# Attention, then a gated feed-forward block: output weights loaded between q and v of batch 1, half of the output of batch 0 as partial sums beside attention 1, q of batches 2 and 3 in one buffer

## The chip, the cores and the metric

One core of one Trainium2 chip runs the whole program. The time is that of one execution on the device in microseconds; the number that counts is the median of the runs of a kernel. "Clock" is the share of TensorE's full clock that was granted. PE is TensorE, DVE VectorE, ACT ScalarE, POOL GpSimd and SP SyncE; POOL and SP here do little but issue DMAs, each in order on its own queue.

## What is computed

Eight batches, 8 heads, 576 positions of 64 numbers, 32 memory slots. The slots are weighted sums of k and v, the queries attend to them, and the 4608 x 512 result goes through a gated feed-forward block:

```python
a = softmax(phi, over the 32 slots)            # [b, h, s, m]
k_m = einsum('bhsm,bhsd->bhmd', a, k)
v_m = einsum('bhsm,bhsd->bhmd', a, v)
attn = softmax(q @ k_m^T / sqrt(64))           # [b, h, s, m]
x = (attn @ v_m), heads side by side           # [4608, 512]
out = (silu(x @ w_gate) * (x @ w_val)) @ w_out # 512 -> 1536 -> 512
```

## The kernel before

**Tiles.** The kernel works batch by batch. The 32 slots of 4 heads fill 128 partitions, so a batch has two groups of heads. `k_items`, `v_items` and `kv_items` sum k and v with the exponentials of phi (`phi_exp`, on ACT) and transpose the sums (`kv_T`). `scores` multiplies them with the transposed q and takes E = exp on ACT. `z_inv` sums E over the slots on PE and takes Ln and Exp on ACT. `norm` multiplies E by that on DVE (t_A). `u_round` multiplies v_m with the columns of w_gate and w_val (t_U), evicted half by ACT and half by DVE, so that x itself is never made.

**Slots.** `gv_slots` has 24 slots for each batch. A slot makes 288 columns of gate and of value for one of the 12 blocks of d_ff, four matmuls in all; ACT takes Silu of the gate and DVE multiplies it with the value into t_h.

**Output units.** `out_units` makes an output tile of 128 rows from 12 matmuls, called units here, one for each block of d_ff, into a PSUM tile of pool `po` (two buffers), evicts it by DVE or ACT (t_o, three buffers) and stores it by two DMAs on SP. An even batch gives 4 such tiles, an odd one 5. They wait in the list `backlog`. At the start of each batch from 2 on, 2 + 8 + 14 + 12 = 36 units are taken between the steps of attention; `rest` is spread among the 24 slots by `spread`, which sorts by a position given by hand. Before, `rest` leaves 36 units in the list in each batch but the last; batch 1 has 12 units beside its slots, batches 2, 4 and 6 have 24, batches 3 and 5 have 12, and batch 7 has 48. The last 60 units run alone.

**Loads.** Weights, phi, k, v and q come through POOL's queue. An issue there waits until the eighth issue ahead of it has landed, and for its buffer to be free. q has two buffers that take turns. From batch 2 on q is transposed by a DMA on SP (`load_qT`); q of batches 0 and 1 by PE (`q_T`). The program text is the order on each engine. `preload_act_table_set` loads a function table on ACT (ACT_TABLE_LOAD).

**Attention 1** is what stands between the slots of batch 0 and those of batch 1. Here no output units run before.

Of the kernel before, what the change touches and what calls it, by code (L numbers as in the profile page):

```python
# [9 lines left out]
FP32 = mybir.dt.float32  # L10
BF16 = mybir.dt.bfloat16
# [3 lines left out]
def kernel(  # L15
# [17 lines left out]
    nc = tc.nc  # L33
    AF = mybir.ActivationFunctionType
    ALU = mybir.AluOpType

    B, H, S, D = q.shape
    M = phi.shape[3]
    DM, DF = moe_w_gate.shape
    P, J = 96, 6  # L40
    NG = 2
    NP = H // 2
    NJF = DF // 128
# [7 lines left out]
    inp = ctx.enter_context(tc.tile_pool(name="inp", bufs=2))  # L51
# [3 lines left out]
    work = ctx.enter_context(tc.tile_pool(name="work", bufs=3))  # L55
    ps = ctx.enter_context(tc.tile_pool(name="ps", bufs=6, space=bass.MemoryType.PSUM))
    po = ctx.enter_context(tc.tile_pool(name="po", bufs=2, space=bass.MemoryType.PSUM))
# [4 lines left out]


    phis, kvs, qs, qTs = {}, {}, {}, {}

    def load_phi(b, eng):
        t = inp.tile([P, H, J * M], FP32, tag="phi", name="t_phi")
        eng.dma_start(out=t, in_=phi[b].rearrange("h (p j) m -> p h (j m)", p=P))  # L68
        phis[b] = t
# [6 lines left out]
    def load_v(b):  # L76
        nc.gpsimd.dma_start(
            out=kvs[b][:, 1], in_=v[b].rearrange("h (p j) d -> p h (j d)", p=P)
        )

    def load_q(b):
        t = inp.tile([P, H, J * D], BF16, tag="q", name="t_q")
        nc.gpsimd.dma_start(out=t, in_=q[b].rearrange("h (p j) d -> p h (j d)", p=P))  # L83
        qs[b] = t

# [27 lines left out]
    WO = {}  # L113

    def load_wo(c):
        t = wpool.tile([128, 4, DM], BF16, tag=f"WO{c}", name=f"WO{c}")
        nc.gpsimd.dma_start(
            out=t,
            in_=moe_w_out[c * CH:(c + 1) * CH, :].rearrange("(i p) f -> p i f", p=128),
        )  # L120
        for i in range(4):
            WO[4 * c + i] = t[:, i]
# [9 lines left out]
    def phi_exp(b):  # L132
        t = att.tile([P, J, NG, NP, M], BF16, tag="ephi", name="t_ephi")
        src = phis.pop(b).rearrange("p (i g) (j m) -> p g i j m", g=NG, m=M)
        for g in range(NG):
            nc.scalar.activation(  # L136
                out=t[:, :, g].rearrange("p j i m -> p i j m"), in_=src[:, g], func=AF.Exp
            )
        ephis[b] = t
# [45 lines left out]
    def v_norm(b, p):  # L185
        bv = att.tile([128, NG, D], BF16, tag="bv", name="t_bv")
        nc.vector.tensor_tensor(
            out=bv,
            in0=p,
            in1=rSs[b].rearrange("p g a c -> p g (a c)").to_broadcast([128, NG, D]),  # L190
            op=ALU.mult,
        )
        bvs[b] = bv
# [43 lines left out]
    def v_items(b):  # L237


        def sums():  # L240
            p = ps.tile([128, NG * D], FP32, tag="b", name="p_kv")
            kv_sum(b, p, (1,))
            v_norm(b, p.rearrange("p (g d) -> p g d", g=NG))

        return [sums, lambda: kv_T(b, (1,))]
# [20 lines left out]
    def gv_banks():  # L266
        return [
            ps.tile([128, CH], FP32, tag="b", name=f"p_{'gv'[r]}") for r in range(2)
        ]

    def scores(b, g):
        p = gv_banks()
        for i in range(NP):
            for r in range(2):
                nc.tensor.matmul(  # L275
                    p[r][32 * i:32 * i + 32, 0:HALF],
                    lhsT=kTs[b][64 * r:64 * r + 64, g, 32 * i:32 * i + 32],
                    rhs=qTs[b, i][64 * r:64 * r + 64, g],
                    start=True,
                    stop=True,  # L280
                    tile_position=(64 * r, 32 * i),
                )
        e = att.tile([128, 2, HALF], BF16, tag=f"E{g}", bufs=1, name="t_E")
        for r in range(2):
            nc.scalar.activation(out=e[:, r], in_=p[r][:, 0:HALF], func=AF.Exp, scale=sm_scale)  # L285
        es[b, g] = e
# [15 lines left out]
    def norm(b, g):  # L302
        a = att.tile([128, 2, HALF], BF16, tag=f"A{g}", name="t_A")
        nc.vector.tensor_tensor(out=a, in0=es.pop((b, g)), in1=lzs.pop((b, g)), op=ALU.mult)  # L304
        atts[b, g] = a
# [33 lines left out]
    hts = {}  # L339
# [48 lines left out]
            t += n  # L388
        return segs

    def out_units(c, u, eng):

        mine = {}

        def unit(jf):
            def run():
                if jf == 0:
                    mine["p"] = po.tile([128, DM], FP32, tag="o", name="p_oo")
                nc.tensor.matmul(  # L399
                    mine["p"],  # L400
                    lhsT=hts[c, jf][:, 128 * u:128 * (u + 1)],
                    rhs=WO[jf],
                    start=(jf == 0),
                    stop=(jf == NJF - 1),
                )
                if jf == NJF - 1:
                    t_o = work.tile([128, DM], FP32, tag="to", name="t_o")
                    if eng == "a":
                        nc.scalar.copy(out=t_o, in_=mine["p"])  # L409
                    else:  # L410
                        nc.vector.tensor_copy(out=t_o, in_=mine["p"])  # L411
                    for (r0, n, bb, jj, pp) in token_segments(2 * c * S + 128 * u, 128):
                        nc.sync.dma_start(
                            out=out_r[bb, jj, pp:pp + n, :], in_=t_o[r0:r0 + n, :]
                        )

            return run

        return [unit(jf) for jf in range(NJF)]

    def out_list(b):
        tiles = range(0, 4) if b % 2 == 0 else range(4, 9)
        res = []
        for n, u in enumerate(tiles):
            res += out_units(b // 2, u, "v" if n % 4 != 3 else "a")
        return res
# [9 lines left out]
    def u_both_halves(b, c, half, evac="avav"):  # L436

        both = ((0, c, (half,)), (1, c, (half,)))
        return lambda: u_round(b, both, evac)
# [4 lines left out]
    def run(items):  # L444
        for x in items:
            x()
# [33 lines left out]
    for c in range(NCH):  # L480
        for half in range(2):
            for which in range(2):
                load_w(which, c, half)
    load_phi(2, nc.gpsimd)
    load_k(1)
    load_q(1)
    load_v(1)
    for c in range(3):
        load_wo(c)


    exp_tables()
# [22 lines left out]


    exp_tables()
    phi_exp(2)
    run(k_items(1)[:2])
    warm(8)  # L520
    run(q_items(1)[:2] + k_items(1)[2:] + q_items(1)[2:])
    load_q(2)
    load_k(2)
    load_v(2)
    load_phi(3, nc.gpsimd)
    load_q(3)
    for g in range(NG):
        scores(1, g)
    for g in range(NG):
        z_inv(1, g)  # L530
    run(v_items(1))
    norm(1, 0)
    run([u_both_halves(1, 0, 0, "vava")])
    nc.scalar.preload_act_table_set("silu_and_others")
    norm(1, 1)
    backlog = out_list(0)

    def take(n):
        nonlocal backlog
        n = max(0, min(n, len(backlog)))  # L540
        part, backlog = backlog[:n], backlog[n:]
        return part

    for b in range(1, B):
        last = b + 1 == B
        if b > 1:
            exp_tables()
            run(take(2))
            for g in range(NG):
                scores(b, g)  # L550
            if not last:
                load_k(b + 1)
                load_v(b + 1)
            if b + 2 < B:
                load_phi(b + 2, nc.gpsimd)
                load_q(b + 2)
            run(take(8))
            if not last:
                phi_exp(b + 1)
            for g in range(NG):  # L560
                z_inv(b, g)
            nc.scalar.preload_act_table_set("silu_and_others")
            run(take(14))
            norm(b, 0)
            norm(b, 1)
            run(take(12))
        rest = take(len(backlog)) if last else take(len(backlog) - 36)
        g = gv_slots(b)
        streams = [(g, 0, 24), (rest, 0, 24)]
        if b == 1:  # L570
            streams += [
                ([u_both_halves(1, 0, 1)], 1, 2),
                ([u_item(1, 1)], 5, 6),
                ([u_item(1, 2)], 10, 11),
            ]
        else:
            streams += [([u_item(b, 2)], 5, 6)]
        if not last:
            n = 6 if b == 1 else 0
            streams += [  # L580
                ([lambda: load_qT(b + 1)], n, n),
                (kv_items(b + 1), 15, 19) if b == 1 else (kv_items(b + 1), 8, 14),
                ([u_item(b + 1, 0)], 18, 20) if b == 1 else ([u_item(b + 1, 0)], 15, 17),
                ([u_item(b + 1, 1)], 21, 23),
            ]
        spread(*streams)
        flush_mul()
        backlog += out_list(b)
# [31 lines left out]
```

## Time and profile before

| what | value |
|---|---|
| median of 3 runs | 271.58 us (270.94 to 271.93) |
| the profiled execution | 270.88 us |
| its span, first to last instruction | 269.1 us |
| mean granted clock | 0.946 |
| PE busy | 246.0 us (91%) |
| ACT busy | 171.0 us (64%) |
| DVE busy | 152.2 us (57%) |
| DMA written, in 48336 packets | 37.00 MB |

The times of rows are microseconds from the start of the span. The two strips show the span in 40 slices of 6.7 us each; a digit is a share in tenths, for PE of busy time, for PEclk of the full clock:

```profile
PE   7576997798829999999999999999999999999993
PEclk9955999689968999999999999999999999999998
```

Slices 7 to 12 cover 40 to 81 us: attention 1, batch 1 and the start of batch 2. Busy time of PE holds the modelled end of each matmul, so a full slice may still have small gaps.

### The profile page before, as it was taken

The numbers are of one execution on the slowest core, as the hardware profiler recorded it, in microseconds if no ns is written. First come the engines' busy times: TensorE is split into PE (matmuls) and PEld (weight loads), VectorE is DVE, ScalarE is ACT, GpSimd is POOL, SyncE is SP. The second block draws the span as 40 slices with busy tenths as digits, with TensorE's granted clock in tenths as the row PEclk, the third lists the DMA queues.
The fourth block names the chain that finished last, engine by engine and source line by source line (L and its number), as shares of the span: only waits on it lengthen the run. The fifth ranks groups of instructions, "written<-read, shape, count | busy, mean of one in ns | idle before, by whom it ended". The sixth has DMA issues, their size and how long they took to land.

```text
span 269.1 us, 6537 instructions
## 1 busy us (share of the span) xinstructions
PE 246.0 (91%) x2574; PEld 146.2 (54%) x2574; DVE 152.2 (57%) x337; ACT 171.0 (64%) x371; POOL 35.9 (13%) x52
## 2 busy tenths in 40 slices
PE   7576997798829999999999999999999999999993
PEld 7442665356404575556645665566556654566541
DVE  0116893576902677558845685478646873565321
ACT  3257788865827556976797568867985677544200
POOL 8435523200022021100210300000000000000000
PEclk9955999689968999999999999999999999999998
DMA  7999999999999979967988596270135102312143
GB/s 150 226 198 196 220 201 206 205 226 144 168 197 174 284 102 181 164 170 128 147 158 221 82 212 126 58 150 0 41 95 115 39 9 72 80 39 73 46 118 78
DMA packets 48336, 37.00 MB, mean 137 GB/s; under 512 B 15921, under 2 KB 42801, under 8 KB 48305
## 3 DMA queue, kind: packets, MB, share of 16 engines
q0 software_dynamic: 27744, 23.01, 54.2%
q1 hardware_dynamic: 20560, 13.57, 23.5%
q8 instruction: 20, 0.33, 0.5%
q14 instruction: 12, 0.09, 0.1%
HBM read 42.47 MB, written 9.44 MB: 193 GB/s over the span
## 4 chain that ended last, share of the span: by engine, by line
PE 69%; DMA 28%; issue 1%; POOL 0%; DVE 0%; POOLq 0%
PE p_oo L399 34%; PE p_g L352 14%; PE p_v L352 13%; DMA t_qT<-t_q 9%; DMA t_kv<-in_k_dram 8%; DMA t_kv<-in_v_dram 6%; DMA W<-in_moe_w_gate_dram 5%; PE p_u L318 3%; PE p_kv L150 1%; PE p_g L275 1%; PE p_kv L162 1%; PE p_g L295 1%; PE p_v L295 1%; POOL t_phi L68 0%; DVE t_o L411 0%
## 5 line engine op out<-in xcount | busy, mean ns | idle before, releaser
L399 PE MATMUL p_oo<-WO,t_h 128*128 128x512 bf16 x432 | 120.1, 385 | 0.0
L368 ACT ACTIVATE t_sg<-p_g 128x288 bf16<-128x288 f32 x192 | 76.9, 415 | 49.8 <-PE p_g L352 46.7
L375 DVE TENSOR_TENSOR t_h<-t_sg,p_v 128x288 bf16<-128x288 bf16 x192 | 84.5, 451 | 35.6 <-PE p_v L352 32.3
L352 PEld LDWEIGHTS <-t_U 128*128 128x128 bf16 x768 | 73.9, 100 | 44.9 <-issue 9.2
L352 PE MATMUL p_g<-t_A,t_U 128*128 128x288 bf16 x384 | 81.3, 294 | 2.7 <-DVE t_A L304 2.1
L352 PE MATMUL p_v<-t_A,t_U 128*128 128x288 bf16 x384 | 79.6, 291 | 0.0
L399 PEld LDWEIGHTS <-t_h 128*128 128x128 bf16 x432 | 42.1, 99 | 36.6 <-issue 4.7
L411 DVE COPY t_o<-p_oo 128x512 f32<-128x512 f32 x28 | 19.3, 688 | 43.7 <-PE p_oo L399 43.7
L336 DVE CAST t_U<-p_u 128x512 bf16<-128x512 f32 (+1 forms) x57 | 32.1, 605 | 1.5 <-PE p_u L318 0.7
L334 ACT CAST t_U<-p_u 128x512 bf16<-128x512 f32 (+1 forms) x55 | 26.3, 530 | 7.5 <-PE p_u L318 7.1
L136 ACT ACTIVATE t_ephi<-t_phi 96x768 bf16<-96x768 f32 x16 | 12.6, 844 | 8.6 <-DMA t_phi<-in_phi_dram 8.6
L318 PE MATMUL p_u<-W,t_kT 64*32 64x512 bf16 (+1 forms) x448 | 16.8, 365 | 0.6 <-DVE t_kT L206 0.6
L83 POOL DMA_DIRECT2D t_q<-in_q_dram x8 | 6.2, 773 | 69.7 <-DMA t_qT<-t_q 66.0
L304 DVE TENSOR_TENSOR t_A<-t_E,t_lz 128x576 bf16<-128x576 bf16 x16 | 11.7, 753 | 3.5 <-ACT t_lz L299 3.5
L409 ACT COPY t_o<-p_oo 128x512 f32<-128x512 f32 x8 | 4.7, 585 | 13.6 <-DMA out_dram<-t_o 10.0
L299 ACT ACTIVATE t_lz<-t_lz 128x576 f32<-128x576 f32 x16 | 10.9, 683 | 0.5
L275 PE MATMUL p_g<-t_qT,t_kT 64*32 64x288 bf16 x64 | 5.1, 321 | 6.3 <-DMA t_qT<-t_q 5.9
L458 ACT ACT_TABLE_LOAD x8 | 10.3, 1283 | 0.9 <-PEq L604 0.7
L285 ACT ACTIVATE t_E<-p_g 128x288 bf16<-128x288 f32 x16 | 6.6, 414 | 6.5 <-PE p_v L275 6.4
L467 PE MATMUL p_oo<-bones 128*128 128x128 bf16 x118 | 8.4, 239 | 1.5 <-DVE bones L478 1.5
L170 DVE RECIPROCAL t_rS<-p_kv 128x2 f32<-128x2 f32 x8 | 1.4, 171 | 14.8 <-PE p_kv L162 14.8
L318 PEld LDWEIGHTS <-t_kT 64*32 64x32 bf16 x448 | 4.5, 89 | 9.1 <-issue 6.6
(42 smaller groups left out, 133.6 us busy)
## 6 DMA issues: line engine op xcount, KB each, us to landing
t_kv<-in_k_dram POOLq DMA_DIRECT2D x8, 576.0 KB, 9.6
t_q<-in_q_dram POOLq DMA_DIRECT2D x8, 576.0 KB, 9.5
t_kv<-in_v_dram POOLq DMA_DIRECT2D x8, 576.0 KB, 13.1
out_dram<-t_o SPq DMA_DIRECT2D x24, 192.0 KB, 2.3
t_phi<-in_phi_dram POOLq DMA_DIRECT2D x7, 576.0 KB, 11.7
out_dram<-t_o SPq DMA_DIRECT2D x24, 128.0 KB, 2.4
W<-in_moe_w_gate_dram POOLq DMA_DIRECT2D x6, 256.0 KB, 12.9
W<-in_moe_w_val_dram POOLq DMA_DIRECT2D x6, 256.0 KB, 11.8
```

The lines of the kernel that those rows point to most:

```text
L136: nc.scalar.activation(out=t[:, :, g].rearrange("p j i m -> p i j m"), in_=src[:, g], func=AF.Exp)
L299: nc.scalar.activation(out=lz, in_=lz, func=AF.Exp, scale=-1.0)
L304: nc.vector.tensor_tensor(out=a, in0=es.pop((b, g)), in1=lzs.pop((b, g)), op=ALU.mult)
L318: nc.tensor.matmul(p[g][32 * i:32 * i + 32, f0:f1], lhsT=kTs[b][64 * g:64 * g + 64, 2, 32 * i:32 * i + 32], rhs=W[which, c][64 * g:64 * g ...
L334: nc.scalar.copy(out=t, in_=p)
L336: nc.vector.tensor_copy(out=t, in_=p)
L352: nc.tensor.matmul(p[:, 0:HALF], lhsT=Us[b, which, c, g][:, 128 * o:128 * (o + 1)], rhs=atts[b, g][:, r], start=(g == 0), stop=(g == NG - 1),)
L368: nc.scalar.activation(out=sg, in_=gate, func=AF.Silu)
L375: nc.vector.tensor_tensor(out=dst, in0=sg, in1=val, op=ALU.mult)
L399: nc.tensor.matmul(mine["p"], lhsT=hts[c, jf][:, 128 * u:128 * (u + 1)], rhs=WO[jf], start=(jf == 0), stop=(jf == NJF - 1),)
L411: nc.vector.tensor_copy(out=t_o, in_=mine["p"])
L458: nc.scalar.preload_act_table_set("natural_log_exp_and_others")
```

## The change

There are four parts.

1. **Load order.** k and q of batch 1 are issued first, then output weights 0 and 1, phi of 2, v of 1, output weight 2. k and v of batch 2 now stand ahead of q of batch 2.
2. **q's buffers.** `Q_SLOT` gives each batch its buffer: batches 0, 2, 3, 5 and 7 use one, batches 1, 4 and 6 the other. q of 3 therefore waits until the transpose of q of 2 has read that buffer.
3. **Output of batch 0.** The first 8 units of output tiles 0 and 1 run in attention 1 (`out_part`); the sum is copied to SBUF by DVE (t_part). The other 4 units run later, and DVE adds the two on eviction. Of tiles 2 and 3 the first 8 units run in attention 1 and the rest in batch 1. phi's exponentials for batch 2 and the table for Silu move behind `z_inv`.
4. **Lists.** `rest` now takes all that is left in `backlog` in each batch, so batch 1 has 16 units beside its slots and batch 7 has 12. The transpose of q of 2 moves from position 6 to 12 of batch 1.

```diff
+    Q_SLOT = (0, 1, 0, 0, 1, 0, 1, 0)
...
-        t = inp.tile([P, H, J * D], BF16, tag="q", name="t_q")
+        t = inp.tile([P, H, J * D], BF16, tag=f"q{Q_SLOT[b]}", bufs=1, name="t_q")
...
-    def out_units(c, u, eng):
+    def out_units(c, u, eng, first=0):
...
-                    if eng == "a":
+                    if first:
+                        nc.vector.tensor_tensor(
+                            out=t_o, in0=mine["p"], in1=parts.pop(u), op=ALU.add
+                        )
+                    elif eng == "a":
...
+    def out_part(u, count):
+        mine = {}
+        def unit(jf):
+            def run():
+                if jf == 0:
+                    mine["p"] = po.tile([128, DM], FP32, tag="o", name="p_oo")
+                nc.tensor.matmul(
+                    mine["p"],
+                    lhsT=hts[0, jf][:, 128 * u:128 * (u + 1)],
+                    rhs=WO[jf],
+                    start=(jf == 0),
+                    stop=(jf == count - 1),
+                )
+                if jf == count - 1:
+                    parts[u] = work.tile([128, DM], FP32, tag=f"part{u}", bufs=1, name="t_part")
+                    nc.vector.tensor_copy(out=parts[u], in_=mine["p"])
...
-    phi_exp(2)
     run(k_items(1)[:2])
     warm(8)
     run(q_items(1)[:2] + k_items(1)[2:] + q_items(1)[2:])
-    load_q(2)
     load_k(2)
     load_v(2)
+    load_q(2)
     load_phi(3, nc.gpsimd)
     load_q(3)
     for g in range(NG):
         scores(1, g)
+    p0, p1 = out_part(0, 8), out_part(1, 8)
+    t2, t3 = out_units(0, 2, "v"), out_units(0, 3, "a")
+    run(p0[:4] + p1[:4])
     for g in range(NG):
         z_inv(1, g)
-    run(v_items(1))
+    phi_exp(2)
+    nc.scalar.preload_act_table_set("silu_and_others")
+    run(p0[4:] + p1[4:])
     norm(1, 0)
+    norm(1, 1)
+    run(t2[:8] + t3[:3] + v_items(1)[:1] + t3[3:6] + v_items(1)[1:] + t3[6:8])
     run([u_both_halves(1, 0, 0, "vava")])
-    nc.scalar.preload_act_table_set("silu_and_others")
-    norm(1, 1)
-    backlog = out_list(0)
+    backlog = t2[8:] + t3[8:] + out_units(0, 0, "v", 8) + out_units(0, 1, "v", 8)
...
-        rest = take(len(backlog)) if last else take(len(backlog) - 36)
+        rest = take(len(backlog))
...
-            n = 6 if b == 1 else 0
+            n = 12 if b == 1 else 0
```

What this does to the order on POOL, from the last gate and value weights on, is seen in these rows (t_kv holds k and v of a batch, WO0 to WO2 are the output weights; the numbers tell the buffers of one name apart). Before:

```order
L68 DMA t_phi_124<-in_phi_dram 96x8x192
L73 DMA t_kv_126<-in_k_dram 96x8x384
L83 DMA t_q_128<-in_q_dram 96x8x384
L77 DMA t_kv_126<-in_v_dram 96x8x384
L117 DMA WO0_131<-in_moe_w_out_dram 128x4x512
L117 DMA WO1_133<-in_moe_w_out_dram 128x4x512
L117 DMA WO2_135<-in_moe_w_out_dram 128x4x512
L83 DMA t_q_960<-in_q_dram 96x8x384
L73 DMA t_kv_962<-in_k_dram 96x8x384
L77 DMA t_kv_962<-in_v_dram 96x8x384
L68 DMA t_phi_965<-in_phi_dram 96x8x192
L83 DMA t_q_967<-in_q_dram 96x8x384
```

The same twelve places now:

```order
L74 DMA t_kv_124<-in_k_dram 96x8x384
L84 DMA t_q_126<-in_q_dram 96x8x384
L118 DMA WO0_128<-in_moe_w_out_dram 128x4x512
L118 DMA WO1_130<-in_moe_w_out_dram 128x4x512
L69 DMA t_phi_132<-in_phi_dram 96x8x192
L78 DMA t_kv_124<-in_v_dram 96x8x384
L118 DMA WO2_135<-in_moe_w_out_dram 128x4x512
L74 DMA t_kv_957<-in_k_dram 96x8x384
L78 DMA t_kv_957<-in_v_dram 96x8x384
L84 DMA t_q_960<-in_q_dram 96x8x384
L69 DMA t_phi_962<-in_phi_dram 96x8x192
L84 DMA t_q_964<-in_q_dram 96x8x384
```

Two output weights have gone ahead of phi of 2 and v of 1, and q of 2 (t_q_960 in both) has gone behind k and v of 2. The last row is q of 3, which now waits for the transpose of q of 2.

On SP the stores and the transposes stand in one queue. Its first rows before (the first is phi of batch 0, t_qT_1204 is q of 2 transposed):

```order
L68 DMA t_phi_87<-in_phi_dram 96x8x192
L89 DMA_TRANSPOSE t_qT_1204<-t_q_960 128x24x96
L413 DMA out_0_dram<-t_o_1525 96x512
L413 DMA out_0_dram<-t_o_1525 32x512
L413 DMA out_0_dram<-t_o_1609 64x512 x2
```

And now:

```order
L69 DMA t_phi_87<-in_phi_dram 96x8x192
L419 DMA out_0_dram<-t_o_1207 32x512
L419 DMA out_0_dram<-t_o_1207 96x512
L419 DMA out_0_dram<-t_o_1325 96x512
L419 DMA out_0_dram<-t_o_1325 32x512
L90 DMA_TRANSPOSE t_qT_1338<-t_q_960 128x24x96
```

The four stores of output tiles 2 and 3 now stand ahead of the first transpose.

On PE, from the last matmul of the scores of batch 1 to its first slot (the rows of t_E are the sums over the slots, p_kv the sums of v, p_T their transpose, p_u0 a U round, p_g and t_A a gate), before:

```order
L275 MATMUL p_v_983<-t_qT_929,t_kT_940 32x288
...
L295 MATMUL p_g_995<-t_E_979,bones_85 128x288
...
L150 MATMUL p_kv_1011<-t_kv_126,t_ephi_141 32x64
...
L200 MATMUL p_T_1062<-ident_84,t_bv_1060 128x128
...
L318 MATMUL p_u0_1067<-W00_106,t_kT_940 32x256
...
L352 MATMUL p_g_1098<-t_A_1065,t_U_1077 128x288
```

And now, up to the U round, with the first row of each group of output matmuls (p_oo, the first two the partial sums):

```order
L276 MATMUL p_v_980<-t_qT_926,t_kT_937 32x288
...
L437 MATMUL p_oo_992<-WO0_128,t_h_488 128x512
...
L437 MATMUL p_oo_997<-WO0_128,t_h_488 128x512
...
L296 MATMUL p_g_1002<-t_E_976,bones_85 128x288
...
L437 MATMUL p_oo_992<-WO1_130,t_h_612 128x512
...
L401 MATMUL p_oo_1038<-WO0_128,t_h_488 128x512
...
L401 MATMUL p_oo_1047<-WO0_128,t_h_488 128x512
...
L151 MATMUL p_kv_1051<-t_kv_124,t_ephi_141 32x64
...
L401 MATMUL p_oo_1047<-WO0_128,t_h_593 128x512
...
L201 MATMUL p_T_1105<-ident_84,t_bv_1100 128x128
...
L319 MATMUL p_u0_1110<-W00_106,t_kT_937 32x256
```

Between the scores and the U round 32 output matmuls have come in: 8 ahead of the sums over the slots, 8 + 8 + 3 behind them, and 3 + 2 beside v.

More of the change, by code (lines that the diff above doesn't have):

```diff
@@ L396, in run @@
             def run():
-                if jf == 0:
+                if jf == first:
                     mine["p"] = po.tile([128, DM], FP32, tag="o", name="p_oo")
@@ L402, in run @@
                     rhs=WO[jf],
-                    start=(jf == 0),
+                    start=(jf == first),
                     stop=(jf == NJF - 1),
@@ L417, in unit @@
             return run
-        return [unit(jf) for jf in range(NJF)]
+        return [unit(jf) for jf in range(first, NJF)]
+    parts = {}
+    def out_part(u, count):
[14 more added lines that the diff above has]
+                    nc.vector.tensor_copy(out=parts[u], in_=mine["p"])
+            return run
+        return [unit(jf) for jf in range(count)]
     def out_list(b):
@@ L483 @@
                 load_w(which, c, half)
-    load_phi(2, nc.gpsimd)
     load_k(1)
     load_q(1)
+    load_wo(0)
+    load_wo(1)
+    load_phi(2, nc.gpsimd)
     load_v(1)
-    for c in range(3):
-        load_wo(c)
+    load_wo(2)
     exp_tables()
```

## The prediction

> **What bounds the kernel now.** I read the chain of work that ended last first, then the windows of the stages that it names, then the waits, the landings of the DMAs and the timeline. Rows of the chain are: start in us, us, what.
>
> ```profile
> 55.73 22.98 DMA t_qT<-t_q
> 78.76 0.42 PE p_g L275
> ...
> 109.32 0.43 PE p_oo L399 x2
> ...
> 121.40 0.56 PE p_u L318 x16
> ...
> 124.45 0.78 PE p_kv L150 x48
> ...
> 135.75 0.43 PE p_oo L399 x2
> ...
> 164.77 0.43 PE p_oo L399 x2
> ...
> 220.21 0.43 PE p_oo L399 x2
> ...
> 251.73 12.96 PE p_oo L399 x60
> ```
>
> From 78.76 on the chain is TensorE alone. Before that it is one transfer, the DMA transpose of q of batch 2, which holds the chain for 23 us. The rows marked x2 are the two output matmuls (0.43 us) that stand just before the scores of batches 3, 4, 5 and 7. Scores to scores, batch 2 takes 109.75 - 78.76 = 30.99 us, batch 3 takes 26.43, batch 4 takes 29.02. Batch 7, from 220.64 to its last slot at 251.73, takes 31.09. Sixty output matmuls in 12.96 us are 0.216 us each at full clock.
>
> Next the windows: length, busy time of PE, weight loads, DVE, ACT and POOL with instruction counts, then the granted clock, DMA share and GB/s.
>
> ```profile
> 40.20:49.20 9.00, 6.05 (x181) 3.86 (x180) 4.07 (x12) 8.27 (x18) 3.01 (x4) 0.97 1.27 205
> 47.00:48.00 1.00, 0.42 (x25) 0.18 (x11) 0.40 (x2) 0.99 (x3) 0.00 (x0) 1.00 1.27 210
> 49.20:55.50 6.30, 5.73 (x36) 2.84 (x37) 2.91 (x7) 3.93 (x10) 1.55 (x2) 0.50 1.30 204
> 40.20:78.76 38.56, 28.39 (x434) 16.97 (x433) 22.09 (x52) 25.16 (x54) 4.57 (x6) 0.88 1.31 190
> 78.76:82.78 4.02, 4.02 (x25) 1.32 (x26) 0.00 (x0) 2.76 (x6) 2.76 (x4) 0.50 0.84 158
> 118.06:135.75 17.69, 17.69 (x220) 11.76 (x219) 14.71 (x34) 12.46 (x30) 2.30 (x3) 1.00 0.83 136
> ```
>
> TensorE's slack lies between the end of batch 0's slots (40.2) and batch 2: 38.56 - 28.39 = 10.2 us idle, and two stretches at half clock. The one from about 48.7 to 55.5 wastes some 2.9 us of its 5.73 busy, the one up to 82.78 wastes 4.02 / 2 = 2.0. In all some 15 us. After 83 there is none: PE fills each window.
>
> **The change, part by part.**
>
> **1. Work moved.** Before, 36 output matmuls of batch 0 are carried from batch to batch and run in batch 7, where PE is the chain. Now 32 run inside attention 1 and 4 more in batch 1's slots (16 units instead of 12). Batches 2 to 6 keep their 36 + 24 or 36 + 12 units. Batch 7 loses 36 x 0.216 = 7.8 us. What could take its place: batch 3's slots, with the same 12 units, are PE-bound at 17.69 us, DVE having 14.71 busy there. Batch 3 does more than batch 7 will (in the chain's rows the 48 k/v sums of the next batch, 0.78, the few matmuls behind them, which I put at half of that, and two more U rounds of 0.56: 2.3), so 26.43 - 2.3 = 24.1 is batch 7 by that measure, against 31.09 - 7.8 = 23.3 by subtraction. The gain is 7.0 to 7.8; I take **7.4**.
>
> **2. The wait for q of batch 2.** Rows: who waited for what, total us, times, longest; the transposes issued at 90.6 and 121.1 with their us to landing; timeline rows of two loads, and the landing of the second (its size, us).
>
> ```profile
> SPq L89 <- DMA t_q<-in_q_dram: 38.9, 1, 38.9
> t_qT<-t_q SPq DMA_TRANSPOSE x1, 8.4
> t_qT<-t_q SPq DMA_TRANSPOSE x1, 5.2
> 79.27 0.77 POOL L83 DMA_DIRECT2D t_q<-in_q_dram  x1 [25.15 <-DMA t_qT<-t_q]
> 80.79 0.77 POOL L77 DMA_DIRECT2D t_kv<-in_v_dram  x1
> t_kv<-in_v_dram POOLq DMA_DIRECT2D x1, 576.0 KB, 12.4
> ```
>
> The transpose waited for q to land, then took 23.0 us while v of 2, phi of 3, q, k, v of 3 and phi of 4 streamed in; later transposes take 8.4 us beside two loads and 5.2 beside none. Now q of 3 shares the buffer of q of 2, so its load waits on POOL for that transpose, and k, v of 3, phi of 4 and q of 4 are queued behind it. Only phi of 3 is left to run beside the transpose. On SP it also moves: it stands behind the stores of output tiles 2 and 3, the second of which ACT evicts at slot 11 to 12 of batch 1 (about 63.5 below). So it is issued at about 64.5 and lands at 70 (5.2) to 73 (8.4). Batch 2 wants it at 74, and the wait is gone. The price of the new POOL wait: the five loads start at about 70. By the rows at 79.27 and 80.79 a q, k, v group ends 80.79 + 12.4 - 79.27 = 13.9 us after its first issue, so v of 3 is in at 84. Batch 2 used it 17.7 us after its scores, which is 91.7 here: cost nothing.
>
> **3. Attention 1.** Timeline rows, then the issue and the landing of the last output weight, and the DVE forms (busy us, mean ns):
>
> ```profile
> 42.70 0.68 PE L252 MATMUL p_q<-ident,t_q 96*128 96x96 bf16 x12 [1.06 <-DMA t_q<-in_q_dram]
> 43.94 0.29 PE L275 MATMUL p_g<-t_qT,t_kT 64*32 64x288 bf16 x1
> 48.17 0.41 PE L318 MATMUL p_u<-W,t_kT 64*32 64x256 bf16 x16 [0.32 <-DVE t_kT L206]
> 48.33 0.68 ACT L299 ACTIVATE t_lz<-t_lz 128x576 f32<-128x576 f32 x1
> 49.17 0.42 PE L352 MATMUL p_g<-t_A,t_U 128*128 128x288 bf16 x1 [0.59 <-DVE t_U L336]
> 49.56 1.28 ACT L534 ACT_TABLE_LOAD   x1
> 64.48 0.85 PE L150 MATMUL p_kv<-t_kv,t_ephi 96*32 96x128 bf16 x48 [0.70 <-DMA t_kv<-in_v_dram]
> 80.44 1.58 ACT L136 ACTIVATE t_ephi<-t_phi 96x768 bf16<-96x768 f32 x2
> 32.45 0.74 POOL L117 DMA_DIRECT2D WO<-in_moe_w_out_dram  x1 [0.59 <-DMA W<-in_moe_w_gate_dram]
> WO<-in_moe_w_out_dram POOLq DMA_DIRECT2D x1, 512.0 KB, 20.3
> L411 DVE COPY t_o<-p_oo 128x512 f32<-128x512 f32 x28 | 19.3, 688 | 43.7 <-PE p_oo L399 43.7
> L304 DVE TENSOR_TENSOR t_A<-t_E,t_lz 128x576 bf16<-128x576 bf16 x16 | 11.7, 753 | 3.5 <-ACT t_lz L299 3.5
> ```
>
> Loads: in the window from 40.2 the DMA engines are full at 205 GB/s, so a weight of 512 KB costs 2.6 us and an input of 576 KB 2.9; the last weight lands at 32.45 + 20.3 = 52.8. The change permutes seven transfers (phi 2, k, q, v of 1, three weights) that still end at 52.8. Counted back from there, v of 1 lands at about 50.2, phi of 2 at 47.3, the second weight at 44.4, the first at 41.8. k and q of 1 come one input (2.9 us) earlier, so the 1.06 us wait for q goes.
>
> PE then: scores from 43.94 - 1.06 = 42.9 to 43.8; eight partial matmuls (1.7) to 45.5, while ACT makes E; four sums for the denominators (0.5) to 46.0; 8 + 8 + 3 matmuls (4.1) to 50.1, while ACT takes Ln and Exp; v sums on v just landed, 0.5; 3 + 2 matmuls (1.1) beside the v chain, to 51.9; U round and first slot 49.17 - 48.17 = 1.0 later, 52.9. I add 0.8 for bank waits: the third and fourth tiles need the banks that the two DVE copies of partial sums (0.69 each) release. First slot at **53.7**. ACT ends its Exp at 48.33 + 0.68 - 0.5 = 48.5, then phi's exponentials 1.58 and the table 1.28, to 51.4: hidden under PE's matmuls by 2 us; beyond that each us counts fully. DVE: two copies, and both output tiles 0 and 1 evicted by an addition that the trace does not show: between the copy, 0.69, and the product of 576 columns, 0.75. I take 0.70, nearest to the copy, which reads the same PSUM tile.
>
> Batch 1's slots: batch 3's 17.69, plus 4 matmuls (0.9), a half and a full U round (0.9), plus 0.8 for DVE, which gets two more evictions and the U casts; its busy time comes to about 18 of 20. That is 20.3, and v of 2 (0.70 wait at 64.48) is loaded one transfer earlier. With dense matmuls from 43.8 on I hold the clock at full. Batch 2's scores come at 53.7 + 20.3 = **74.0**, 4.8 earlier than 78.76. With good luck 52.8 + 19.6 = 72.4, with bad 54.5 + 21.4 = 75.9.
>
> **4. Clock of batch 2.** No idle stretch ahead of it: the 2.0 us lost at half clock up to 82.78 come back. Check: batch 2 minus batch 4, which does the same work, is 30.99 - 29.02 = **2.0**.
>
> **Sum.** 4.8 + 2.0 + 7.4 = 14.2 us. The profiled execution took 270.88 (span 269.1 and 1.8 around it): 256.7. The median of the runs is 0.70 above it, 271.58: **257.4**. The bounds of the terms (6.4 + 2.0 + 7.8 and 2.9 + 2.0 + 7.0) give 255.4 to 259.7. This fits the 15 us of slack counted first: nearly all of it must be used.
>
> **Rivals.**
>
> *Half clock in attention 1.* The 24 transposes and the small scores just before the new matmuls could leave the clock to drop at about 45, for as long as the 6.8 us it was low before. Half of 6.8 us of dense matmuls is lost, 3.4 us: 260.8. Against it stands the window from 47 to 48: the same transposes and scores had just run, thinner than now, and the clock was still 1.00. In favour: it was 0.97 over the whole stretch, so the fall came right behind. 10%.
>
> The Trainium skill says on its page "TensorE: Matmul & The Clock Gate" (Part 4, PE-mode transpose) that transposes on TensorE do not count as busy for the clock gate as matmuls do. By that rule this rival would be likelier; the window just quoted, at 1.00 after those transposes, does not bear it out.
>
> *The loads bind attention 1.* v of 1 lands at 50.2 only if the queue keeps its pace; PE reaches it at 50.1. One weight more (2.6 us) in its way moves every later step by that: 260.0. For it: no margin at all, and the DMA share is 1.27 there. Against: the order of the seven does not change their sum. 10%.
>
> *The end does not shrink.* If the matmuls in batch 7 had been cover for waits of its gate and value chain, half of 7.4 would come back: 261.1. Against: batch 3. 4%.
>
> *The transpose is late, slower than before.* If it needs 23.0 us again, for instance because descriptors and not the competing loads slow it, it lands at about 65 + 23 = 88, 9.2 later than 78.76; PE idles, batch 2 starts cold as before, and only 7.4 comes back: 273.4. It decides once the transpose takes more than 74 - 64.5 = 9.5 us, and passes 271.6 when it takes over about 22. Against: 8.4 and 5.2 in lighter traffic. 3%.
>
> **How the numbers follow.** The forecast, 257.4, has 73%. The range 254.8 to 261.6 holds the bounds of the sum, half a us below them, and the first three rivals; what it leaves out is the late transpose and a miss of several terms at once. A measurement of this kernel tells about 0.5% (1.4 us) from no change. Faster by more than that: 0.95; within it: 0.02; slower: 0.03.
>
> **What would show it.** Right: PE's window 44 to 53 almost full at clock 1.00; no idle time of PE before the scores of batch 2, at 73 to 75; POOL waiting on q of 3 until about 70; the transpose of q of 2 in under 9 us; batch 7 some 7.4 us shorter, and the last sixty matmuls unchanged. Wrong: a half clock between 45 and 56, PE waiting for v of 1 or the third weight, a transpose that lands after 74, or PE idle in batch 7.

## The result, and the profile after

The changed kernel takes 262.73 us (median; 261.92 to 264.62) where the kernel before takes 271.75 on the same chips: the ratio is 0.9676, 95% interval 0.9615 to 0.9738. It is faster, as forecast, but by 9.0 us instead of 14.2, and the time lies above the range. The profiled execution took 262.94 us, its span 261.1, 8.0 less than before.

Where the 8.0 us came from is best seen from batch to batch. Each column is the time from the first matmul of one batch's scores to that of the next, read from the timeline of PE; the last is from batch 7's scores to the end of the span.

| kernel | 1 to 2 | 2 to 3 | 3 to 4 | 4 to 5 | 5 to 6 | 6 to 7 | 7 to end |
|---|---|---|---|---|---|---|---|
| before | 34.82 | 30.93 | 26.42 | 29.02 | 26.43 | 29.02 | 48.5 |
| after | 31.33 | 32.45 | 28.04 | 29.34 | 26.43 | 29.34 | 40.9 |

Attention 1 and batch 1 got shorter, though they hold 36 more matmuls, and the end by 7.6. Batches 2 and 3, forecast at 29.0 and 26.4, took 3.4 and 1.6 us too long.

First the part that went as foreseen. Rows of the timeline after (start, us, engine, line, what, and in brackets the idle time ahead and what ended it; SPq is the DMA queue of SP), then one window of attention 1 and the landing of the transpose issued at 64.72:

```profile
51.19 0.55 PE L151 MATMUL p_kv<-t_kv,t_ephi 96*32 96x64 bf16 x48 [0.23 <-DMA t_kv<-in_v_dram]
53.77 0.42 PE L353 MATMUL p_g<-t_A,t_U 128*128 128x288 bf16 x2 [0.44 <-DVE t_U L337]
64.72 3.07 SPq L90 DMA_TRANSPOSE t_qT<-t_q  x1
44.00:53.00 9.00, 8.52 (x101) 4.05 (x110) 3.23 (x6) 6.75 (x13) 0.00 (x0) 1.00 1.25 201
t_qT<-t_q SPq DMA_TRANSPOSE x1, 6.5
```

The first slot of batch 1 starts at 53.77 (foreseen: 53.7), PE is busy 8.52 of 9 us at full clock, and the transpose of q of 2 lands in 6.5 us, long before batch 2 wants it at 74.6.

Then the part that did not. The chain after and the waiting matmul behind it; the windows around that; POOL's issues from the timeline; the landings of the transpose of q of 3 and of the last load:

```profile
80.20 2.75 PE p_oo L401 x12
...
84.62 22.36 DMA t_qT<-t_q
107.03 0.42 PE p_g L276
107.70 3.21 PE p_oo L401 x8
```

```profile
103.46:107.03 3.57, 0.00 (x2) 0.01 (x2) 0.87 (x2) 0.85 (x1) 0.00 (x0) 1.00 0.75 208
107.03:110.50 3.47, 3.47 (x23) 1.19 (x24) 0.00 (x0) 2.76 (x6) 2.29 (x3) 0.51 0.42 42
```

```profile
71.77 0.77 POOL L84 DMA_DIRECT2D t_q<-in_q_dram  x1 [27.86 <-DMA t_qT<-t_q]
72.53 0.77 POOL L74 DMA_DIRECT2D t_kv<-in_k_dram  x1
73.29 0.77 POOL L78 DMA_DIRECT2D t_kv<-in_v_dram  x1
74.05 0.79 POOL L69 DMA_DIRECT2D t_phi<-in_phi_dram  x1
74.83 0.78 POOL L84 DMA_DIRECT2D t_q<-in_q_dram  x1
75.59 0.78 POOL L74 DMA_DIRECT2D t_kv<-in_k_dram  x1
76.35 0.78 POOL L78 DMA_DIRECT2D t_kv<-in_v_dram  x1
78.58 0.78 POOL L69 DMA_DIRECT2D t_phi<-in_phi_dram  x1 [1.45 <-ACT t_lz L299]
```

```profile
t_phi<-in_phi_dram POOLq DMA_DIRECT2D x1, 576.0 KB, 28.2
t_qT<-t_q SPq DMA_TRANSPOSE x1, 22.4
```

This is the old picture one batch later. The transpose of q of 3 holds the chain for 22.4 us, PE stands still for 3.57 us, and batch 3 begins at half clock (0.51). The rows of POOL show why one may suspect the loads: when the transpose of q of 2 lands, eight loads go out within 7 us, q, k, v of 3 and phi of 4, and right behind them q, k, v of 4 and phi of 5. Before, the first four had gone out by 54 us, so that only the second four waited for that transpose (the row at 79.27 in the prediction). The last lands at 78.58 + 28.2 = 106.8, the transpose of q of 3, issued at 84.62 in the middle of them, at 107.0.

### The profile page after: what moved, and what is told of

Its sections match the earlier page's. It is cut to its first block, busy times and chain, and to the rows that moved or that the text cites. A ratio compares the mean times of both kernels' runs of the same rounds, so it can differ in the third digit from the quotient of the medians.

```text
span 261.1 us, 6501 instructions
## 1 busy us (share of the span) xinstructions
PE 240.3 (92%) x2539; PEld 145.1 (56%) x2574; DVE 154.7 (59%) x339; ACT 171.1 (66%) x371; POOL 35.9 (14%) x52
## 4 chain that ended last, share of the span: by engine, by line
PE 72%; DMA 21%; DVE 3%; issue 2%; POOL 1%; ACT 1%; DVEq 0%; POOLq 0%
PE p_oo L401 30%; PE p_g L353 16%; PE p_v L353 14%; DMA t_qT<-t_q 9%; DMA t_kv<-in_v_dram 7%; DMA t_q<-in_q_dram 5%; PE p_u L319 4%; PE p_kv L151 2%; PE p_g L276 1%; PE p_v L296 1%; PE p_g L296 1%; PE p_q L253 1%; PE p_kv L163 1%; DVE t_h L376 1%; POOL t_phi L69 1%
## 5 line engine op out<-in xcount | busy, mean ns | idle before, releaser
L401 PE MATMUL p_oo<-WO,t_h 128*128 128x512 bf16 x382 | 104.6, 383 | 0.7 <-issue 0.5
L353 PEld LDWEIGHTS <-t_U 128*128 128x128 bf16 x768 | 73.0, 99 | 40.8 <-issue 9.0
L353 PE MATMUL p_g<-t_A,t_U 128*128 128x288 bf16 x384 | 79.7, 290 | 3.2 <-DVE t_A L305 1.6
L353 PE MATMUL p_v<-t_A,t_U 128*128 128x288 bf16 x384 | 78.4, 288 | 0.0
L401 PEld LDWEIGHTS <-t_h 128*128 128x128 bf16 x416 | 40.4, 99 | 36.7 <-issue 4.0
L417 DVE COPY t_o<-p_oo 128x512 f32<-128x512 f32 x26 | 18.0, 691 | 45.7 <-PE p_oo L401 43.8
L335 ACT CAST t_U<-p_u 128x512 bf16<-128x512 f32 (+1 forms) x55 | 26.4, 530 | 9.1 <-PE p_u L319 8.6
L137 ACT ACTIVATE t_ephi<-t_phi 96x768 bf16<-96x768 f32 x16 | 12.6, 843 | 9.0 <-DMA t_phi<-in_phi_dram 9.0
L151 PE MATMUL p_kv<-t_kv,t_ephi 96*32 96x128 bf16 (+1 forms) x480 | 7.6, 214 | 2.1 <-DMA t_kv<-in_k_dram 1.6
```

The source lines that it names most:

```text
L137: nc.scalar.activation(out=t[:, :, g].rearrange("p j i m -> p i j m"), in_=src[:, g], func=AF.Exp)
L151: nc.tensor.matmul(p[32 * i:32 * i + 32, n * g:n * (g + 1)], lhsT=ephis[b][:, j, g, i], rhs=kvs[b][:, w0:w1, 2 * i + g, j * D:(j + 1) * D] ...
L335: nc.scalar.copy(out=t, in_=p)
L353: nc.tensor.matmul(p[:, 0:HALF], lhsT=Us[b, which, c, g][:, 128 * o:128 * (o + 1)], rhs=atts[b, g][:, r], start=(g == 0), stop=(g == NG - 1),)
L401: nc.tensor.matmul(mine["p"], lhsT=hts[c, jf][:, 128 * u:128 * (u + 1)], rhs=WO[jf], start=(jf == first), stop=(jf == NJF - 1),)
```

## The experiments

**q of all batches from 2 on in one buffer.** If the stack of loads is the cause, q of 4 must be held back until q of 3 is transposed.

```diff
-    Q_SLOT = (0, 1, 0, 0, 1, 0, 1, 0)
+    Q_SLOT = (0, 1, 0, 0, 0, 0, 0, 0)
```

> Changed kernel, but q of all batches from 2 on shares one buffer, so that the load of q of 4 (and all that is queued behind it on POOL: k and v of 4, phi of 5) waits for the transpose of q of 3. Theory A (the transpose of q of 3 is slow because eight loads were stacked beside it): that transpose falls from 22.4 us to under 10, PE's 3.6 us wait before the scores of batch 3 goes and with it the half clock behind it (1.6 us): 262.7 - 3.4 - 1.6 = about 257.7 us. Rival B (it is slow for another reason: the stores beside it on SP, its place, its late source): the transpose stays at about 22 us and the time at 262 to 263. Rival C: the later loads come too late for batch 3 (k/v sums, scores of 4) and a new wait of 2 us or more appears there.

Measured: 258.07 us, ratio to the kernel before 0.9478 (0.9423 to 0.9533). POOL's second q, k, v, phi now starts at 93.17, and the transpose of q of 3 needs 7.4 us:

```profile
93.17 0.77 POOL L84 DMA_DIRECT2D t_q<-in_q_dram  x1 [17.67 <-DMA t_qT<-t_q]
t_qT<-t_q SPq DMA_TRANSPOSE x1, 7.4
```

Batches 2 and 3 take 29.02 and 26.43 us, as batches that wait for nothing do. Stores, place and source of the transpose are unchanged, so theory A holds and B falls; no new wait appears in later batches (C).

**Two loads beside it.** The same, with k and v of 4 ahead of the waiting load of q of 4.

```diff
             if b + 2 < B:
                 load_phi(b + 2, nc.gpsimd)
+                if b == 2:
+                    load_k(4)
+                    load_v(4)
                 load_q(b + 2)
```

(and `load_k`, `load_v` of 4 left out of batch 3.)

> As the kernel with one buffer, but k and v of 4 are issued ahead of q of 4, so that they run beside the transpose of q of 3 while q of 4 and phi of 5 do not. A dose between none and four. Theory A: what is left in the queue at its issue (about 0.9 of v of 3, 3.0 phi of 4, 2.9 + 2.9) and 5.2 of its own give about 15 us; it lands some 4 us before batch 3 wants it, so the time equals that of the one-buffer kernel, about 257.7. Rival B: 22 us again and a wait; or under 9 us, if the loads beside it do not count.

Measured: 257.64 us, 0.9476 (0.9420 to 0.9531), not to be told from the one-buffer kernel. The transpose of q of 3:

```profile
t_qT<-t_q SPq DMA_TRANSPOSE x1, 16.1
```

16.1 us between 7.4 and 22.4, against 15 expected: the time of the transpose follows the loads beside it, and it still landed 3 us before the scores of batch 3, so it cost nothing.

**q's buffers taking turns as before.**

```diff
-    Q_SLOT = (0, 1, 0, 0, 1, 0, 1, 0)
+    Q_SLOT = (0, 1, 0, 1, 0, 1, 0, 1)
```

> Changed kernel, but q's two buffers take turns as before (q of 3 does not wait for the transpose of q of 2; q of 4 does). Theory A: q, k, v of 3 and phi of 4 now run beside the transpose of q of 2, about 11.5 us of loads left at its issue at 64.7 and 5.2 of its own: it lands at 81 to 83, batch 2 waits 6 to 8 us for it and starts at half clock (2 us); the wait of batch 3 goes (5 us): about 266 to 267 us. Rival: the shared buffer does nothing, 262.7.

Measured: 269.16 us (median of ten, 267.01 to 270.93 and one of 272.16), 0.9897 (0.9857 to 0.9937). The profiled execution, one of 267.01, shows the wait and the transpose of q of 2:

```profile
PE p_g L276 <- DMA t_qT<-t_q: 8.0, 1, 8.0
t_qT<-t_q SPq DMA_TRANSPOSE x1, 17.9
```

PE waits 8.0 us in batch 2, and batch 3 needs its 26.43 again. The traced execution, the fastest of the ten, fits the forecast; the median is some 2 us above it and the runs spread by 4 to 5 us, more than those of the other changed kernels. The three fastest have a mean granted clock of 0.957 or 0.958, the others 0.941 to 0.954; what sets that apart is open.

**Output weights late.** The loads of attention 1 in their old order.

```diff
+    load_phi(2, nc.gpsimd)
     load_k(1)
     load_q(1)
-    load_wo(0)
-    load_wo(1)
-    load_phi(2, nc.gpsimd)
     load_v(1)
-    load_wo(2)
+    for c in range(3):
+        load_wo(c)
```

> Changed kernel, but with the loads of attention 1 in their old order (phi of 2, k, q, v of 1, then the three output weights). The weights then land at about 47.7, 50.2 and 52.8 instead of 42, 44.5 and 52.8. If the early weights are what lets the 32 matmuls fill attention 1, PE waits about 3.5 us for the first weight right after the scores and may fall to half clock: 266 to 269 us. Rival: the waits are hidden elsewhere (q of 2's transpose, batch 3's wait): 262.7.

Measured: 267.11 us, 0.9826 (0.9772 to 0.9881), 4.4 more than the changed kernel. Right behind the scores PE waits for the first weight:

```profile
48.19 1.89 PE L437 MATMUL p_oo<-WO,t_h 128*128 128x512 bf16 x7 [2.62 <-DMA WO<-in_moe_w_out_dram]
44.00:53.00 9.00, 6.02 (x49) 2.94 (x47) 1.70 (x5) 5.12 (x13) 0.46 (x1) 1.00 1.26 205
```

PE has 6.02 us of work in that window instead of 8.52; the clock does not fall. Not all of the 4.4 us belongs to the weights: in the old order phi of 2 also stands ahead of k and q of 1, and the scores of batch 1 start 1.1 us later (44.36 instead of 43.25). From there to the scores of batch 2 the kernel takes 34.04 us instead of 31.33. These 2.7 us are about the wait for the first weight: the filled attention 1 needs the early weights.

**The buffers alone.** The kernel before, with `Q_SLOT` as in the change and nothing else.

> The kernel before with nothing changed but the buffers of q (batches 0, 2, 3, 5, 7 in one, 1, 4, 6 in the other). Theory A: the load of q of 3, with k, v of 3, phi of 4 and q of 4 behind it, now waits for the transpose of q of 2, which then has only k, v of 2 and phi of 3 beside it (8.8 us of loads) and takes about 14 us instead of 23.0; it lands at about 70, ahead of the end of batch 1's slots (72.9), so the 5.9 us wait and the 2.0 us of half clock behind it go. But the loads of batch 4 stack up beside the transpose of q of 3, which takes about 22 us: some 5 us come back at batch 3. In all 271.8 - 7.9 + 5 = about 269 us. Rival: the wait of batch 2 stays (its own place at slot 6 or its order in the queue sets it), 271.8 or more.

Measured: 267.60 us, 0.9869 (0.9801 to 0.9936). Its transposes of q of 2 and q of 3:

```profile
t_qT<-t_q SPq DMA_TRANSPOSE x1, 12.6
t_qT<-t_q SPq DMA_TRANSPOSE x1, 23.4
```

The wait of batch 2 goes, with the transpose at its old place (1 to 2 takes 28.29 instead of 34.82), and the stack comes back at batch 3: 2 to 3 takes 33.34 and 3 to 4 28.11. Both are due to the buffers alone.

**One buffer alone.** The kernel before, with one buffer for q from batch 2 on and nothing else.

> The kernel before with nothing changed but one buffer for q of all batches from 2 on. Theory A: as with the buffers alone, but no stack beside the transpose of q of 3, so no wait in batch 3: 271.8 - 7.9 = about 264 us. The rest of the way to the changed kernel with one buffer (258) is then what the moved output work brings, about 6 us. Rival: the two parts need each other (one buffer without the filled attention 1 brings less than 5 us, because the loads of batch 3 come too late for a batch 2 that starts earlier): 267 us or more.

Measured: 262.62 us, 0.9691 (0.9642 to 0.9740): as fast as the whole change. The transpose of q of 3 takes 6.9 us. Beside the changed kernel with one buffer this shows what the other parts of the change, the moved output with the loads and places that go with it, cost and bring together. Windows from the scores of 1 to the scores of 2, first this kernel, then the changed one with one buffer:

```profile
43.21:72.59 29.38, 25.88 (x337) 14.80 (x339) 18.94 (x44) 21.46 (x51) 3.17 (x5) 0.83 1.07 160
```

```profile
43.37:75.20 31.83, 29.58 (x370) 16.79 (x374) 21.53 (x48) 22.93 (x53) 3.41 (x5) 1.00 0.97 169
```

36 matmuls, 7.8 us at full clock, lengthen the stretch by 2.45 us: they stand where PE was idle, and the clock rises from 0.83 to 1.00. The 2.45 is uncertain by about 1 us: the buffers-alone kernel, which is the same program up to there, took 28.29 us for this stretch, at a mean clock of 0.88. Batches 4 and 6 take 0.32 us longer each, and the end is 7.6 us shorter. That leaves 4.5 us, where the medians 262.62 and 258.07 differ by 4.55 and about 6 was forecast; that it agrees so closely is in part chance.

## Why the prediction was wrong

**Work moved: right.** The end got 7.6 us shorter, against 7.4. Batch 7's slots were bound by PE, and nothing took the place of the 36 matmuls.

**The wait for q of batch 2: right as far as it goes.** The transpose was issued at 64.72 (foreseen 64.5) and took 6.5 us; the wait was gone, and the clock of batch 2 was full. The two-buffer kernel shows that the shared buffer does this, not the later place: at the same place, with the loads beside it, the transpose takes 17.9 us and PE waits 8.0. With the buffers alone, at the old place, the wait is gone as well.

**The price of that wait: the step that failed.** The prediction listed "k, v of 3, phi of 4 and q of 4" behind the waiting load of q of 3, checked that v of 3 comes in time, and put the cost at nothing. It did not follow the queue past q of 4. Before, q of 4 was the load that waited for the transpose of q of 2. In the new plan q of 3 waits for it, one group of loads earlier, and q of 4 takes the other buffer, which has long been free. So nothing holds POOL back between the two groups, and k, v of 4 and phi of 5 follow at once. The prediction had priced a transpose among stacked loads itself (23.0 us), named it a rival for q of 2 with 3%, and had not asked the same of q of 3, the next transpose on the same queue. With the length of batch 2 set at 29.02 and of batch 3 left as it was, 3.4 + 1.6 = 5.0 us were missing: what was put at nothing cost 5.0 us. Taking the stack away, and nothing else, gave 258.07, within 0.7 of the 257.4 that was forecast.

**Attention 1: right, the first slot partly by luck.** It came at 53.77 for 53.7, batch 2's scores at 74.58 for 74.0. The gain of this term was 4.2 instead of 4.8, mostly because batch 1's slots took 20.8 us and not 20.3. On the way to the first slot two misses cancel: PE reached the sums of v 0.9 us later than foreseen (50.96 for 50.1), and the 0.8 us put aside for bank waits was not needed, as no output matmul of attention 1 waits for a bank in the trace. The loads bound it hardly: v of 1 landed at 51.15 for 50.2, and PE waited 0.23 us for it. The rival of the half clock did not come: the clock was 1.00 from 44 to 53, right behind the 24 transposes.

**Not foreseen:** 0.32 us each in batches 4 and 6 of all kernels with the moved output, in the sums over the slots (`z_inv`). The traces before and after show that these sums now wait for E: in batch 4 the last of them starts 0.05 us after E is done. The lists meet these batches at another tile, so the last output tile ahead of them is evicted by ACT (0.60 us) and no longer by DVE, and ACT ends E of batch 4 2.75 us after the first matmul of the scores instead of 2.26. No run tests this by moving that eviction back.

By terms, foreseen and measured in the profiled executions: attention 1 4.8 and 4.2; batch 2's clock 2.0 and, with the new wait, -1.5; batch 3 none and -1.6; batches 4 and 6 none and -0.6; the end 7.4 and 7.6. The measured ones sum to 8.1, the spans differ by 8.0.

## What to carry to other kernels

A wait in a DMA queue is also a throttle. When a buffer plan removes it, follow the queue to the next wait that is left, count what now goes out together, and look for the transfer on another queue that will run among it. A transfer that is slow because of its neighbours has to be priced by what is in flight at its issue, each time it occurs. Work that fills idle time of TensorE can pay twice: it shortens the stage it came from, and here it also kept the clock up.

## What the runs showed of the hardware

How strongly the loads on POOL's queue slow a DMA transpose on SP's was not expected. The loads still to land at its issue were counted from the landings; the rest of one that is nearly in counts as 0.3.

| kernel, transpose | loads beside it | us |
|---|---|---|
| after, q of 2 | none | 6.5 |
| one buffer, q of 3 | 1.3 | 7.4 |
| after, q of 4 | 2 | 8.9 |
| buffers alone, q of 2 | 3 | 12.6 |
| two loads, q of 3 | 3.3 | 16.1 |
| two buffers, q of 2 | 4 | 17.9 |
| after, q of 3 | 5.3 | 22.4 |
| before, q of 2 | 7 | 23.0 |

It is no straight line. Up to two loads cost the transpose little, about 1 us each; from two to 5.3 each adds some 4 us (22.4 - 8.9 over 3.3), and from there to seven nearly nothing. Though on a queue of its own, beside 3.3 to 5.3 loads it ends 0.2 to 1.7 us after the last of the loads issued ahead of it; beside seven it ends 2.8 us before the last. The Trainium skill says in "DMA: Bandwidth & Descriptors" (Queues, rings and completion order) that each DMA engine takes turns between its queues, a packet at a time. The row of seven loads agrees that neither queue waits for the other to be empty; that the transpose should come off so badly in those turns the page does not say, and why it does was not measured here.
